# Router logits and prefix sums as 64-row halves, added on VectorE

## The chip, the cores and the metric

The kernel runs on one core of a Trainium2 chip. The metric is the device time of one execution in microseconds (us), the median of several. A core has five engines with a queue each: PE (TensorE: matmuls, with weight loads shown apart as PEld), DVE (VectorE), ACT (ScalarE), POOL (GpSimd) and SP (SyncE, here only issuing DMAs). Matmul results go to PSUM, eight banks of 2 KiB per partition.

## The reference

Two parts, one after the other. Attention without softmax, over 8 batches of 2816 tokens with 256 features and 64 query/key features:

```python
scores = (1.0 / S) * np.matmul(z, z.transpose(0, 2, 1))
attn = np.maximum(scores, 0.0) ** 2
x = (u * np.matmul(attn, v)).reshape(B * S, D)
```

Then a dense layer and a mixture of 8 experts, of which each token uses one:

```python
y_dense = np.maximum(x @ w1_dense, 0.0) @ w2_dense
logits = x @ w_gate                      # (22528, 8)
expert_idx = np.argmax(logits, axis=1)
gate_w = softmax(logits)[rows, expert_idx]
y[mask_e] = y_dense[mask_e] + gate_w[mask_e] * (np.maximum(x[mask_e] @ w1[e], 0.0) @ w2[e])
```

## The kernel before

The 22528 tokens are 176 blocks of 128. The attention takes them two at a time. For a query group of two or four blocks, `scores` multiplies z with itself into a pair of PSUM banks (L406); one of ACT and DVE applies the scaled relu (L421, L423) and one of ACT, DVE or, in the first groups, POOL squares into a bf16 tile `A` (L434, L436). `av` multiplies `A` with v into another pair of banks (L604), and DVE multiplies by u into `pays` (`gate_x`, L631). Since the query/key width is 64, z lies in SBUF twice, on rows 0 to 63 and on rows 64 to 127, and every matmul of the attention uses 64 rows of the 128x128 array: two matmuls stand side by side, one on each half of the rows, each with a PSUM bank of its own. The profile writes such a matmul as 64*128 and one over all rows as 128*128. v is used in the same halves, so a pair of L604 matmuls sums over 128 keys. There are four pairs of banks in the attention. `touch` is a tiny 64-row matmul by which `swap_rows` exchanges the two halves' banks in the middle of a block (L552).

For routing, the blocks form 18 chunks: 14 of 11 blocks, then 8, 6, 4 and 4. Each finished pair of blocks is transposed by a DMA on SP's queue into `xT` (L633). When a chunk is complete, `routing` runs in two steps put between the attention's matmuls. `logits` takes a pair of banks and does two matmuls per block, one for each 128 of the 256 features, with `xT` as weights and the eight router columns streamed (L660); `route_a` finds on DVE the largest logit and the one-hot choice `oh` (L670 to L680), and ACT takes the exponential. `route_pre` makes two 128-row matmuls of `oh` (L690, L691), with a matrix of ones and with a strict triangle; `route_b` turns them on DVE, in three functions `one`, `two`, `three`, into each token's place in its expert's list (L704 to L730). `scatter` then writes each block's rows to that place in DRAM by an indirect DMA on POOL (L748, L750). The last two chunks of 4 blocks are routed after the attention in PSUM tiles of another kind.

The order of the instructions on PE, ACT, DVE and SP is written out by a planner in the kernel while it is being built. It keeps an estimated time `now` along PE's work, and a time from which each other engine is free. Operations are offered with a readiness time, a rank and an estimated duration for each engine that may run them; the earliest possible start wins, then the lower rank. `route_a` and the three functions of `route_b` are such offers, for DVE alone, at ranks 0 and 0.5; relus have rank 1 and squares rank 4. Logits advance `now` by 0.6 us and the prefix sums by 0.25 us. A pair of banks goes back to the list when the last function that reads it is estimated to be done. On the chip the engines follow that order and wait on semaphores; the durations only shape the order.

After the attention, 90 slots (two more if the lists need them) fetch 256 sorted rows each, run the dense layer and the expert (L962, L970), combine on ACT and DVE (L985, L986), and POOL scatters the result into the output (L988).

Of the kernel before, what the change touches and what calls it, by code (L numbers as in the profile page):

```python
# [15 lines left out]
P = 128  # L16
# [3 lines left out]
def kernel(  # L20
# [12 lines left out]
    nc = tc.nc  # L33
    B, S, D = u.shape
    dq = z.shape[2]
    E = moe_w_gate.shape[1]
# [5 lines left out]
    G = 11  # L42
    sizes = [G] * (nB // G - 2) + [8, 6, 4, 4]
    starts = [sum(sizes[:q]) for q in range(len(sizes) + 1)]
    assert nK % G == 0 and starts[-1] == nB
    nQ = len(sizes)
# [37 lines left out]
    def banks(x, name, shape=(P, 2, 4 * P), dt=F32):  # L84

        return ps.tile(list(shape), dt, name=name, tag=f"b{x}")
# [4 lines left out]
    wg = const.tile([P, 2, E], BF, name="wg")  # L91
    w1d = const.tile([P, 2, F], BF, name="w1d")
    w2d = const.tile([P, 4, D], BF, name="w2d")
    ones = const.tile([P, P], BF, name="ones")
    ntri = const.tile([P, P], BF, name="ntri")
# [39 lines left out]
    now = [0.0]  # L135
# [5 lines left out]
    z_of, zn_of, zT_of, v_of, ut_of, xT_of, lg_of, rs = {}, {}, {}, {}, {}, {}, {}, {}  # L141
# [132 lines left out]
    for b in range(B):  # L274
        i = 0
# [14 lines left out]
    def offer(ready, rank, ways, then=None):  # L290
        count[0] += 1
        todo.append((rank, count[0], ready, ways, then))
# [91 lines left out]
    def take_pair():  # L384
        return pairs.pop(0)[1]

    def give_pair(t, x):
        pairs.append((t, x))
        pairs.sort()
# [249 lines left out]
    def vec(name, a, b=1, dt=F32, **kw):  # L639

        t = rt.tile([P, G * E if b > 1 else G], dt, name=name, **kw)
        return t[:, :a * b].rearrange("p (a b) -> p a b", b=b) if b > 1 else t[:, :a]

    bank_of = {}

    def small(q, name, shape):
        if q < nQ - 2:
            return banks(bank_of[q], name, shape)
        tag = "y" if q == nQ - 2 else "s"
        return late[tag].tile(list(shape), F32, name=name, tag=tag)  # L650

    def logits(q):
        n = sizes[q]

        lg = small(q, "lg", (P, G, E))
        lg_of[q] = lg[:, :n, :]
        for j in range(n):
            xT = xT_of.pop(starts[q] + j)
            for c in range(2):
                nc.tensor.matmul(out=lg[:, j, :], lhsT=xT[:, c, :],  # L660
                                 rhs=wg[:, c, :], start=(c == 0), stop=(c == 1))

    def bc(ap2):
        return ap2.unsqueeze(2).to_broadcast([P, ap2.shape[1], E])

    def route_a(q):
        n = sizes[q]
        lg = lg_of.pop(q)
        m = vec("m", n)
        nc.vector.tensor_reduce(out=m, in_=lg, axis=AX.X, op=ALU.max)  # L670
        d = vec("d", n, E)
        nc.vector.tensor_sub(d, lg, bc(m))
        ex = vec("ex", n, E)
        nc.scalar.activation(ex, d, AF.Exp)
        c = vec("c", n, E)
        nc.vector.scalar_tensor_tensor(out=c, in0=d, scalar=0.0, in1=desc8[:, :n, :],
                                       op0=ALU.is_ge, op1=ALU.mult)
        nc.vector.tensor_reduce(out=m, in_=c, axis=AX.X, op=ALU.max)
        oh = vec("oh", E, n, BF)
        nc.vector.tensor_tensor(out=oh.rearrange("p e t -> p t e"), in0=c,  # L680
                                in1=bc(m), op=ALU.is_equal)
        rs[q] = (oh, ex)
# [2 lines left out]

    def route_pre(q):
        oh, ex = rs[q]
        pre = small(q, "pre", (P, 2, E * G))
        pre = [pre[:, i, :E * sizes[q]].rearrange("p (e t) -> p e t", e=E) for i in range(2)]
        nc.tensor.matmul(out=pre[0], lhsT=ones[:], rhs=oh, start=True, stop=True)  # L690
        nc.tensor.matmul(out=pre[1], lhsT=ntri[:], rhs=oh, start=True, stop=True)  # L691
        rs[q] = (oh, ex, pre)

    first_of = [0]
# [1 line left out]
    def route_b(q):  # L696

        n = sizes[q]
        oh, ex, pre = rs[q]
        inc = vec("inc", E, n)  # L700

        def one():
            se = vec("se", n)
            nc.vector.tensor_reduce(out=se, in_=ex, axis=AX.X, op=ALU.add)  # L704
            o = starts[q] % (2 * G)
            rows = pays[:, o:o + n, :]
            nc.vector.reciprocal(rows.bitcast(F32)[:, :, P], se)
            nc.vector.tensor_copy(rows.bitcast(I32)[:, :, P + 1], tok[:, starts[q]:starts[q + 1]])
            assert q != Q1 or made_first[0]
            if first_of[0] != n:  # L710

                first_of[0] = n
                nc.vector.memset(smask[:, :E * n], 1.0)
                nc.vector.memset(smask[:, :E * n].rearrange("p (e t) -> p e t", e=E)[:, :, 0], 0.0)

        def two():
            tb = vec("tb", E, n)
            nc.vector.tensor_copy(tb, pre[0])
            nc.vector.tensor_add(tb[:, :, 0], tb[:, :, 0], base[:])
            nc.vector.tensor_tensor_scan(  # L720
                out=inc.rearrange("p e t -> p (e t)"), data0=smask[:, :E * n],
                data1=tb.rearrange("p e t -> p (e t)"),
                initial=0.0, op0=ALU.mult, op1=ALU.add)
            nc.vector.tensor_copy(base[:], inc[:, :, n - 1])

        def three():
            nc.vector.tensor_add(inc, inc, pre[1])
            nc.vector.tensor_mul(inc, inc, oh)
            pos = vec("pos", n, bufs=5)
            nc.vector.tensor_reduce(out=pos, in_=inc.rearrange("p e t -> p t e"),  # L730
                                    axis=AX.X, op=ALU.add)
            rs[q] = pos

        return [one, two, three]

    def nodep(ins, mine, *groups_):
# [26 lines left out]
    done = const.tile([P, E], F32, name="done")  # L763
# [283 lines left out]
    for b in range(B):  # L1047
        t = b * nK
# [30 lines left out]
    def chain(t, fns, then):  # L1079

        def done(t):
            if fns[1:]:
                chain(t, fns[1:], then)
            else:
                then(t)

        offer(t, 0.5, {"dve": (0.8, lambda eng: fns[0]())}, done)

    def routing(q):
        def first():  # L1090
            bank_of[q] = take_pair()
            logits(q)
            now[0] += 0.6
            offer(now[0] + 0.2, 0, {"dve": (1.3, lambda eng: route_a(q))}, middle)

        def middle(t):
            give_pair(t, bank_of[q])
            jobs.append((t + 2.5, second))

        def second():  # L1100
            bank_of[q] = take_pair()
            route_pre(q)
            now[0] += 0.25
            chain(now[0] + 0.2, route_b(q), last)

        def last(t):
            give_pair(t, bank_of[q])
            routed.append(q)
            waiting.extend(range(starts[q], starts[q + 1]))

        jobs.append((now[0], first))

    def late_routing(q):
        logits(q)
        route_a(q)

    def late_places(q):
        route_pre(q)
        for fn in route_b(q):
            fn()  # L1120
        waiting.extend(range(starts[q], starts[q + 1]))

    LAG = 5
    for q in range(nQ - 2):
        t = starts[q + 1] - 1 + LAG
# [40 lines left out]
    for s in range(NT - MAYBE + 2):  # L1166
# [4 lines left out]
        if s % 3 == 1 and waiting:  # L1171
# [5 lines left out]
    n = nc.values_load(used[0:1, 0:1], min_val=0, max_val=NH,  # L1177
                       skip_runtime_bounds_check_because="made by the table")
# [34 lines left out]
```

## Time and profile before

| | |
|---|---|
| median of 3 runs | 910.43 us (910.18 to 918.82) |
| the profiled execution | 923.2 us, its span 921.5 us, TensorE clock 0.997 |
| PE busy / DVE busy / ACT busy / POOL busy, whole span | 94% / 73% / 76% / 53% |
| first and last attention matmul (L604) | 10.1 us and 557.9 us |
| first matmul of the second part (L962) | 559.9 us |
| routing matmuls in the attention | 336 at L660, 16 at L690, 16 at L691 |

The profile lists instructions by source line. A line of the timeline has the start in us, the length in us, the engine, the line, what it writes and reads, the shape, and how many of the same were merged; in brackets stands the idle time before it and what ended that. A matmul's length contains its passage through the array, so matmuls that follow each other overlap; their pace is read from their starts.

### The profile page before, as it was taken

What the parts mean: (1) busy time and instruction counts of PE and PEld (TensorE: products, weight loads), DVE (VectorE), ACT (ScalarE), POOL (GpSimd) and SP (SyncE); (2) the same over time, 40 slices, a digit from 0 to 9 for tenths busy, and PEclk for the clock granted to TensorE, in tenths of its full rate; (3) what the DMA queues carried; (4) which work ended last, traced back from release to release, by engine and by line L of the source; (5) the groups of instructions that cost most, each with busy time, mean ns of one, the idle gap of its engine ahead of it and who ended that gap; (6) DMA issues with size and microseconds to landing.
All of it is one profiled execution on the core that took longest, in us unless ns stands there. A gap on an engine that the chain in (4) does not pass through costs nothing. (4 is left out here: it accounts for less than half of the span.)

```text
span 921.5 us, 30231 instructions
## 1 busy us (share of the span) xinstructions
PE 868.8 (94%) x12194; PEld 756.0 (82%) x12194; DVE 670.3 (73%) x1295; ACT 696.7 (76%) x868; POOL 485.7 (53%) x532
## 2 busy tenths in 40 slices
PE   7999999999999999999999998989988998999995
PEld 5898798788888888889888887778877887888785
DVE  7998889789889889789889966455634444445554
ACT  8988789789789779779779954567656666766664
POOL 8203353353343363353344344777777877876564
PEclk9999999999999999999999999999999999999998
DMA  9999999999999999999999964755544554443333
GB/s 178 159 198 159 187 189 178 186 185 181 208 161 195 192 185 177 201 183 179 195 167 157 162 129 92 124 123 108 113 102 99 117 110 100 111 101 93 87 90 76
DMA packets 291310, 136.80 MB, mean 148 GB/s; under 512 B 258910, under 2 KB 266334, under 8 KB 291168
## 3 DMA queue, kind: packets, MB, share of 16 engines
q1 hardware_dynamic: 263552, 79.40, 52.6%
q0 software_dynamic: 27616, 55.44, 26.8%
q8 instruction: 96, 1.57, 0.8%
q14 instruction: 46, 0.38, 0.2%
HBM read 61.54 MB, written 37.16 MB: 107 GB/s over the span
## 5 line engine op out<-in xcount | busy, mean ns | idle before, releaser
L604 PE MATMUL o<-vb,A 64*128 64x256 bf16 x7184 | 460.3, 269 | 3.2 <-POOL A L436 1.6
L604 PEld LDWEIGHTS <-A 64*128 64x128 bf16 x7184 | 379.1, 94 | 44.0 <-issue 3.4
L750 POOL DMA_INDIRECT xs<-pays,pi x176 | 192.0, 1091 | 271.9 <-DVE pi L748 218.4
L421 ACT ACTIVATE r<-s 128x1024 f32<-128x1024 f32 x252 | 249.7, 1018 | 40.0 <-PE s L406 33.7
L965 ACT ACTIVATE ring<-h_ps 128x1024 bf16<-128x1024 f32 x180 | 185.5, 1032 | 94.8 <-PE h_ps L962 50.2
L434 ACT ACTIVATE A<-r 128x1024 bf16<-128x1024 f32 (+1 forms) x234 | 238.3, 1045 | 8.2 <-DMA wall<-A 5.3
L986 DVE SCALAR_TENSOR_TENSOR ring<-yy,me,ring 128x256 f32<-128x256 f32 x180 | 86.2, 482 | 158.4 <-ACT ring L985 87.3
L436 DVE TENSOR_TENSOR A<-r 128x1024 bf16<-128x1024 f32 x155 | 187.0, 1220 | 4.6 <-ACT r L421 2.9
L988 POOL DMA_INDIRECT out_dram<-ring,me x140 | 146.1, 1044 | 67.5 <-DVE ring L986 35.4
L970 PEld LDWEIGHTS <-ring 128*128 128x128 bf16 x1440 | 139.9, 98 | 47.5 <-issue 31.9
L423 DVE TENSOR_SCALAR r<-s 128x1024 f32<-128x1024 f32 (+1 forms) x145 | 173.7, 1206 | 6.5 <-PE s L406 3.3
L406 PE MATMUL s<-zT 64*128 64x512 bf16 (+1 forms) x874 | 146.2, 355 | 5.3 <-ACT r L421 1.7
L970 PE MATMUL yy<-w2d,ring 128*128 128x256 bf16 x720 | 107.9, 272 | 24.5 <-DVE ring L986 22.8
L970 PE MATMUL yy<-ring 128*128 128x256 bf16 x720 | 108.0, 273 | 0.0
L962 PE MATMUL h_ps<-ring,w1d 128*128 128x256 bf16 x720 | 94.3, 272 | 3.5 <-DVE pays L631 1.8
L962 PE MATMUL h_ps<-ring 128*128 128x256 bf16 (+1 forms) x880 | 95.3, 253 | 1.4 <-issue 0.8
L985 ACT COPY ring<-yy 128x256 f32<-128x256 f32 x180 | 68.1, 378 | 37.2 <-PE yy L970 18.8
L950 DVE COPY ring<-wall 128x2048 bf16 x110 | 81.4, 755 | 14.5 <-issue 7.7
L962 PEld LDWEIGHTS <-ring 128*128 128x128 bf16 x880 | 73.4, 98 | 12.0 <-DVE ring L950 3.1
L631 DVE TENSOR_TENSOR pays<-o,ut 128x512 bf16<-128x512 f32 x88 | 60.4, 686 | 29.8 <-PE o L604 28.8
L962 PEld LDWEIGHTS <-w1d 128*128 128x128 bf16 x720 | 70.0, 98 | 12.2 <-issue 4.1
L406 PEld LDWEIGHTS <-zT 64*128 64x128 bf16 x874 | 54.9, 94 | 24.1 <-issue 13.7
(122 smaller groups left out, 444.8 us busy)
## 6 DMA issues: line engine op xcount, KB each, us to landing
ut<-in_u_dram SPq DMA_DIRECT2D x88, 256.0 KB
vb<-in_v_dram POOLq DMA_DIRECT2D x16, 384.0 KB
vb<-in_v_dram POOLq DMA_DIRECT2D x16, 320.0 KB
wall<-in_moe_w_dram POOLq DMA_DIRECT2D x16, 256.0 KB
xs<-pays,pi POOLq DMA_INDIRECT x176
zr<-in_z_dram POOLq DMA_DIRECT2D x7, 352.0 KB
out_dram<-ring,me POOLq DMA_INDIRECT x140
ring<-xs SPq DMA_TRANSPOSE x114
```

The source lines that it names most:

```text
L406: nc.tensor.matmul(out=s[:, h, y * c:(y + 1) * c], lhsT=zT[r, k + h, :], rhs=zT[r, i0:i0 + w, :], start=True, stop=True)
L421: nc.scalar.activation(r[:, :, :c], s[:, :, :c], AF.Relu, scale=1.0 / S)
L423: nc.vector.tensor_scalar(out=r[:, :, :c], in0=s[:, :, :c], scalar1=1.0 / S, scalar2=0.0, op0=ALU.mult, op1=ALU.max)
L434: nc.scalar.activation(a, r, AF.Square)
L436: (nc.gpsimd if eng == "pool" else nc.vector).tensor_mul(a, r, r)
L604: nc.tensor.matmul(out=o[:, j, 0:D], lhsT=block(n, k, i + j - i0)[r], rhs=v_of[b][r, k, :], start=(p == 0 and x == 0), stop=(p == 1 and x ...
L750: ins = nc.gpsimd.indirect_dma_start(out=xs, out_offset=bass.IndirectOffsetOnAxis(ap=pi[:], axis=0), in_=pays[:, g % (2 * G), 0:ROW].bitca ...
L962: nc.tensor.matmul(out=h_ps[:, f, hs, :], lhsT=w1(c, f), rhs=xT[:, hs, c, :], start=(c == 0), stop=(c == 1))
L965: nc.scalar.activation(h, h_ps[:].rearrange("p f h t -> p f (h t)"), AF.Relu)
L970: nc.tensor.matmul(out=y[:, k, :], lhsT=h[:, f, j * P:(j + 1) * P], rhs=w2(f), start=(f == 0), stop=(f == 3))
L986: nc.vector.scalar_tensor_tensor(out=ys, in0=y[:, 1, :], scalar=me[:, j, 0:1], in1=yd, op0=ALU.mult, op1=ALU.add)
L988: ins = nc.gpsimd.indirect_dma_start(out=out, out_offset=bass.IndirectOffsetOnAxis(ap=ids[j], axis=0), in_=ys, in_offset=None, bounds_chec ...
```

## The change

In the 16 chunks that are routed during the attention, each 128-row matmul of the logits and of the prefix sums becomes two 64-row matmuls, on rows 0 to 63 and 64 to 127. The first half writes to the first bank of the pair, the second to the second bank. VectorE adds the halves: for the logits a copy from PSUM and an add; for the sums with ones an add more; for the sums with the triangle an add more. The planner's estimate of `route_a` goes from 1.3 to 1.7 us and that of each function of `route_b` from 0.8 to 0.95 us. The last two chunks stay at 128 rows.

```diff
+    def halves(q):
+        return [slice(0, dq), slice(dq, 2 * dq)] if q < nQ - 2 else [slice(0, P)]
     def logits(q):
         n = sizes[q]
-        lg = small(q, "lg", (P, G, E))
-        lg_of[q] = lg[:, :n, :]
+        lg = small(q, "lg", (P, 1, G * E))
+        lg_of[q] = [lg[:, h, :n * E].rearrange("p (n e) -> p n e", e=E) for h in range(lg.shape[1])]
...
             for c in range(2):
-                nc.tensor.matmul(out=lg[:, j, :], lhsT=xT[:, c, :],
-                                 rhs=wg[:, c, :], start=(c == 0), stop=(c == 1))
+                for r, out in zip(halves(q), lg_of[q]):
+                    nc.tensor.matmul(out=out[:, j, :], lhsT=xT[r, c, :],
+                                     rhs=wg[r, c, :], start=(c == 0), stop=(c == 1))
     def route_a(q):
-        lg = lg_of.pop(q)
+        lg, *more = lg_of.pop(q)
         m = vec("m", n)
+        d = vec("d", n, E)
+        for part in more:
+            nc.vector.tensor_copy(d, lg)
+            nc.vector.tensor_add(d, d, part)
+            lg = d
         nc.vector.tensor_reduce(out=m, in_=lg, axis=AX.X, op=ALU.max)
-        d = vec("d", n, E)
         nc.vector.tensor_sub(d, lg, bc(m))
...
     def route_pre(q):
-        nc.tensor.matmul(out=pre[0], lhsT=ones[:], rhs=oh, start=True, stop=True)
-        nc.tensor.matmul(out=pre[1], lhsT=ntri[:], rhs=oh, start=True, stop=True)
+        for w, outs in zip((ones, ntri), pre):
+            for r, out in zip(halves(q), outs):
+                nc.tensor.matmul(out=out, lhsT=w[r, :], rhs=oh[r], start=True, stop=True)
...
         def two():
-            nc.vector.tensor_copy(tb, pre[0])
+            nc.vector.tensor_copy(tb, pre[0][0])
+            for part in pre[0][1:]:
+                nc.vector.tensor_add(tb, tb, part)
...
         def three():
-            nc.vector.tensor_add(inc, inc, pre[1])
+            for part in pre[1]:
+                nc.vector.tensor_add(inc, inc, part)
...
-        offer(t, 0.5, {"dve": (0.8, lambda eng: fns[0]())}, done)
+        offer(t, 0.5, {"dve": (0.95, lambda eng: fns[0]())}, done)
...
-            offer(now[0] + 0.2, 0, {"dve": (1.3, lambda eng: route_a(q))}, middle)
+            offer(now[0] + 0.2, 0, {"dve": (1.7, lambda eng: route_a(q))}, middle)
```

More of the change, by code (lines that the diff above doesn't have):

```diff
@@ L647, in small @@
         if q < nQ - 2:
-            return banks(bank_of[q], name, shape)
+            return banks(bank_of[q], name)
         tag = "y" if q == nQ - 2 else "s"
         return late[tag].tile(list(shape), F32, name=name, tag=tag)
+    def halves(q):
+        return [slice(0, dq), slice(dq, 2 * dq)] if q < nQ - 2 else [slice(0, P)]
     def logits(q):
         n = sizes[q]
-        lg = small(q, "lg", (P, G, E))
-        lg_of[q] = lg[:, :n, :]
+        lg = small(q, "lg", (P, 1, G * E))
+        lg_of[q] = [lg[:, h, :n * E].rearrange("p (n e) -> p n e", e=E) for h in range(lg.shape[1])]
         for j in range(n):
@@ L687, in route_pre @@
         oh, ex = rs[q]
[L688 to L691, printed above, removed]
+        pre = small(q, "pre", (P, 1, 2 * E * G))
+        pre = [[pre[:, h, i * E * G:i * E * G + E * sizes[q]].rearrange("p (e t) -> p e t", e=E)
+                for h in range(pre.shape[1])] for i in range(2)]
+        for w, outs in zip((ones, ntri), pre):
+            for r, out in zip(halves(q), outs):
+                nc.tensor.matmul(out=out, lhsT=w[r, :], rhs=oh[r], start=True, stop=True)
         rs[q] = (oh, ex, pre)
```

## Prediction

> **What bounds the kernel now.** I read first the page's busy times in 40 slices, to see which engine is full in which stretch.
>
> ```profile
> PE   7999999999999999999999998989988998999995
> ...
> DVE  7998889789889889789889966455634444445554
> ACT  8988789789789779779779954567656666766664
> ```
>
> The first 24 slices are the attention, and there PE is full. A busy PE isn't yet a PE at its pace, so the next views are the window from the first to the last attention matmul (columns: stretch, length, then the busy time and count of PE, PEld, DVE, ACT and POOL; granted clock, DMA share, GB/s), and the waits of PE up to 560 us (total, times, longest).
>
> ```profile
> 10.12:558.20 548.08, 536.28 (x9066) 468.22 (x9067) 481.29 (x888) 458.85 (x500) 223.18 (x225) 1.00 1.03 178
> ```
>
> ```profile
> PE d L552 <- ACT r L421: 2.0, 2, 1.7
> ...
> PE s L406 <- ACT r L421: 1.7, 7, 0.3
> PE o L604 <- POOL A L436: 1.6, 3, 0.9
> PE s L406 <- PE s L406: 1.5, 7, 0.3
> ...
> PE o L604 <- ACT A L434: 1.1, 2, 0.6
> ...
> PE o L604 <- DMA vb<-in_v_dram: 0.5, 1, 0.5
> PE pre L690 <- ACT r L421: 0.4, 1, 0.4
> PE s L406 <- DVE r L423: 0.4, 2, 0.2
> ```
>
> The clock is full, 1.00, and these waits sum to 9.2 us in 548: PE's own stream sets the length of the attention. DVE has 548.1 - 481.3 = 66.8 us to spare there, ACT 89.2 us. What the stream's pace is, and what the routing costs it, is read from the timeline around the first chunk, PE and then weight loads, and from the groups of the attention (the number behind the comma is the mean length in ns).
>
> ```profile
> 64.10 0.40 PE L604 MATMUL o<-vb,wall 64*128 64x256 bf16 x4
> 64.43 0.71 PE L660 MATMUL lg<-wg,xT 128*128 128x8 bf16 x22
> 65.07 2.36 PE L604 MATMUL o<-vb,A 64*128 64x256 bf16 x40
> ```
>
> ```profile
> 64.43 0.62 PEld L660 LDWEIGHTS <-xT 128*128 128x128 bf16 x22 [0.21 <-issue]
> ```
>
> ```profile
> L604 PE MATMUL o<-vb,A 64*128 64x256 bf16 x7134 | 456.9, 269 | 2.0 <-ACT A L434 1.1 <-POOL A L436 0.9
> ...
> L660 PE MATMUL lg<-wg,xT 128*128 128x8 bf16 x336 | 10.9, 167 | 0.0
> ...
> L660 PEld LDWEIGHTS <-xT 128*128 128x128 bf16 x336 | 9.5, 96 | 3.4 <-issue 3.4
> ```
>
> One L604 matmul lasts 269 ns; 40 of them, 20 pairs, start within 2.36 - 0.27 = 2.09 us, so a pair is due every 2.09 / 19 = 0.110 us. The two pairs from 64.10 give way at 64.32, but the next L604 starts at 65.07: the chunk's logits take 0.75 us of PE's time. A logit matmul lasts 167 ns, so 22 of them step by (0.71 - 0.167) / 21 = 0.0259 us, and 22 steps are 0.57 us. The other 0.18 us are the way in and out. "issue" says that PE waited for nobody there.
>
> That the gap belongs to the change of shape, not to a change of line or bank, shows where scores stand between L604 matmuls, all of 64 rows:
>
> ```profile
> 70.23 0.38 PE L604 MATMUL o<-vb,wall 64*128 64x256 bf16 x4
> 70.45 0.38 PE L406 MATMUL s<-zT 64*128 64x512 bf16 x2
> 70.67 0.60 PE L604 MATMUL o<-vb,wall 64*128 64x256 bf16 x8
> ```
>
> Two pairs of 256 columns, then one pair of 512, and each group starts 0.22 us after the last: no gap.
>
> **The change part by part.** *Logits, PE.* 22 matmuls of 128 rows become 44 of 64, in pairs on different rows. If the pairs stand side by side as the attention's do, 22 steps of 0.0259 us remain and the 0.18 us go, since no change of shape is left. In the smaller chunks the steps are fewer, and the way in and out is taken to be the same: 16 x 0.18 = 2.9 us saved. The pace of such short pairs isn't in the trace. Its bounds: one step a pair (2.9 us saved), or one step a matmul, which adds 22 x 0.0259 us to a full chunk. The nearest rows are what follows the prefix sums, weight loads and matmuls:
>
> ```profile
> 70.00 0.11 PEld L604 LDWEIGHTS <-A 64*128 64x128 bf16 x4
> ```
>
> ```profile
> 67.76 2.13 PE L604 MATMUL o<-vb,A 64*128 64x256 bf16 x36
> 69.82 0.21 PE L690 MATMUL pre<-oh,ones 128*128 128x88 bf16 x1
> 69.86 0.21 PE L691 MATMUL pre<-oh,ntri 128*128 128x88 bf16 x1
> 70.00 0.39 PE L604 MATMUL o<-vb,A 64*128 64x256 bf16 x4
> ```
>
> Four 64-row loads are done in 0.11 us. The 128-row ones, 96 ns each, step by (0.62 - 0.096) / 21 = 0.025 us, and four would take 3 x 0.025 + 0.096 = 0.17 us. Four matmuls of 0.27 us fit in 0.39, so with 0.110 between the pairs the two of a pair start within 0.01 us of each other. Loads and matmuls of the two halves run side by side, so I take the first bound.
>
> *Prefix sums, PE.* 36 matmuls from 67.76 are 18 pairs, due to give way at 67.76 + 18 x 0.110 = 69.74; the stream resumes at 70.00: 0.26 us per chunk. L691 starts 0.04 us after L690, so two pairs of halves are 0.08 us. Saved: 0.18 x 16 = 2.9 us, and with the logits **5.8 us**.
>
> *VectorE.* Four operations are added per chunk, a copy and three adds of 128x88. Their kinds are in these rows:
>
> ```profile
> 71.05 0.24 DVE L718 COPY tb<-pre 128x88 f32<-128x88 f32 x1
> ...
> 72.11 0.24 DVE L727 TENSOR_TENSOR inc<-inc,pre 128x88 f32<-128x88 f32 x1
> 72.39 0.25 DVE L728 TENSOR_TENSOR inc<-inc,oh 128x88 f32<-128x88 f32 x1
> 72.67 0.31 DVE L730 TENSOR_REDUCE pos<-inc 128x11 f32<-128x88 f32 x1
> ```
>
> A step of such a chain is 0.28 us from start to start, so a chunk has 4 x 0.28 = 1.1 us more, and 16 chunks 17.9 us (somewhat less in the two smaller ones). The maximum and the subtraction now read SBUF in place of PSUM, at no gain: the maximum L670 reads PSUM, L678 reads SBUF, and both take 241 ns.
>
> ```profile
> L670 DVE TENSOR_REDUCE m<-lg 128x11 f32<-128x88 f32 (+2 forms) x16 | 3.9, 241 | 19.3 <-PE lg L660 19.2
> L678 DVE TENSOR_REDUCE m<-c 128x11 f32<-128x88 f32 (+2 forms) x16 | 3.9, 241 | 0.6
> ```
>
> What hides this is the 66.8 us that DVE has idle, and ACT's 89.2, to which the planner can move relus and squares. Without that cover each microsecond is PE's. Behind the added operations stand, on DVE's queue, relus and squares (for which PE waits, through the banks and `A`), `gate_x` (for which the transposes to `xT` wait on SP's queue, and behind these SP's transposes of `A`), and the scatters' casts, for which POOL waits in any case. The logits' banks are last read by the second operation, the add, as they were by the subtraction, so they aren't held longer; those of the prefix sums are held two operations longer, 0.56 us.
>
> How much of DVE's routing reaches PE now? For this chunk it runs from 65.20 to 67.45 and from 71.05 to 72.67 + 0.31 = 72.98:
>
> ```profile
> 65.20 0.24 DVE L670 TENSOR_REDUCE m<-lg 128x11 f32<-128x88 f32 x1
> ...
> 67.38 0.07 DVE L714 MEMSET smask<- 128x8 f32 x1
> ```
>
> That is 2.25 + 1.93 = 4.2 us, 67 us in 16 chunks. The waits of PE for relus, squares and banks, without POOL's, are 2.0 + 1.7 + 1.5 + 1.1 + 0.4 + 0.4 = 7.1 us. If the routing caused all of them, 7.1 / 67 = 11% of a DVE microsecond would reach PE, 1.9 us of the 17.9. Bounds: nothing, if these waits come from elsewhere, and all 17.9. I take **1.5 us**, near the 1.9, because the planner's estimates grow too, by 0.4 + 3 x 0.15 = 0.85 us a chunk against 1.1, so it places other work around most of it.
>
> *The plan.* With other durations the planner picks other engines and places. That changes the 9.2 us of waits either way; I allow 3 us up and down.
>
> *After the attention.* The second part begins when the last `gate_x` is done:
>
> ```profile
> 559.92 1.03 PE L962 MATMUL h_ps<-ring,w1d 128*128 128x256 bf16 x8 [1.79 <-DVE pays L631]
> ```
>
> So what the attention saves moves the end by as much; the second part is unchanged.
>
> **The sum.** -5.8 + 1.5 = -4.3 us. The profiled execution took 923.2 us (its span 921.5 and 1.7 around it) and would take 918.9. It lies 12.8 us above the median of 910.43; where, one profile can't say, but the terms come from a stretch at full clock with a regular pace, so I take them off the median as they are: **906.1 us**.
>
> **The rivals.** *One step a matmul.* If the short halves follow each other, 672 steps of 0.0259 us are 17.4 us, where 336 steps and 2.9 us are 11.6 us now: 5.8 us more. The prefix sums have four steps of 0.04, 0.16 us in place of 0.26, and save 1.6. With DVE's 1.5 the sum is +5.7, 916.1 us. For it: no row has a long run of short 64-row pairs. Against it: the loads and starts at 70.00. Chance 15%. [...]
>
> *VectorE becomes what PE waits for.* If relus queue behind the routing and the banks run out, each of the 17.9 us that passes to PE counts in full. This is the rival on the other side: the loss decides from 5.8 / 17.9 = 32% on; with a half of it the time is 913.5 us, with all of it 910.4 - 5.8 + 17.9 = 922.5. For it: DVE is the fuller of the two engines that empty the banks. Against it: 11% is the most that the waits allow, and the longest of them isn't DVE's, as the next rows show. Chance of more than 32%: 17%, a third of that over 919.5 us.
>
> *The gain is given back at once.* The DMA engines, at a share of 1.03 in the window, hold the attention; then only DVE's 1.5 us count, 911.9 us. For it: PE's longest wait stands behind ACT, which had waited for a transposing DMA.
>
> ```profile
> 172.11 1.06 ACT L434 ACTIVATE A<-r 128x1024 bf16<-128x1024 f32 x1 [3.24 <-DMA wall<-A]
> ...
> 174.13 0.16 PE L552 MATMUL d<-ones 64*128 64x8 bf16 x1 [1.66 <-ACT r L421]
> ```
>
> Against it: that happens once, and PE's own waits for DMA are 0.5 us. The same time results if the change doesn't do what it says and the gaps stay with the 64-row halves, which the scores at 70.45 speak against. Chance together 11%.
>
> *A luckier plan.* The 5.8 us go and more than 3.3 us of the waits too: under 901.3 us. Chance 7%.
>
> **How the numbers follow.** The forecast, 906.1 with a range of its own of 901.5 to 910, has the remaining 50%. A change of 1% (9.1 us) is about what a measurement of this kernel can tell from none. Faster by over 1% is the luckier plan and a little of the forecast's edge, 8%; slower by over 1% is a third of the VectorE rival and the first rival with more waits, 10%; the rest, 82%, is within 1%. The range leaves out the luckier plan below and the upper half of the VectorE rival above: 901.5 to 917.
>
> **What would show it.** Right: 64-row logits with no "issue" gap ahead of their loads, the stream resuming 0.57 us after the pair before gave way, the attention ending near 554 us in the profile, DVE some 15 us busier in it. Wrong: logits that take 1.1 us a chunk; PE's waits for r, A or banks well over 9 us; or a shorter attention and a second part longer by as much.

## The result, and the profile after

The changed kernel takes **920.16 us** (median of 14 runs, 915.33 to 928.0); the kernel before, beside it on the same chip, takes 913.92 us (14 runs, 910.18 to 918.82). The ratio is 1.0065, with a 95% interval of 1.0039 to 1.009: slower by 0.65%, some 6 us, where 4.3 us less were forecast. The time lies above the range's upper end of 917 us. Two of the 12 runs of the kernel with only the logits halved, its profiled one among them, and one of the four runs of that kernel's attention fell into a slower state (894.66, 902.29 and 578.04 us), and the times given below leave them out.

The profiled execution of the changed kernel took 915.33 us, the lowest of its 14; that of the kernel before, 923.2 us, lies above all of its 14. So the two spans can't be held against each other; what PE does in each stretch can. First the window from the first attention matmul to the first matmul of the second part, and from there to the end, of the kernel before and then of the changed kernel (columns as in the prediction):

```profile
10.12:559.90 549.78, 536.28 (x9066) 468.22 (x9067) 482.01 (x890) 458.85 (x500) 223.50 (x225) 1.00 1.03 178
559.90:921.49 361.59, 325.55 (x3060) 283.05 (x3059) 181.46 (x395) 231.54 (x362) 254.29 (x288) 0.99 0.46 103
```

```profile
10.45:561.30 550.85, 533.77 (x9436) 477.56 (x9433) 493.16 (x951) 462.06 (x503) 251.07 (x224) 1.00 1.04 177
561.30:913.59 352.29, 324.80 (x3060) 284.21 (x3059) 183.84 (x396) 231.51 (x362) 255.18 (x289) 0.99 0.44 106
```

The attention is 1.1 us longer, though PE is busy for 2.5 us less in it and DVE for 11 us more. The second part, with the same matmuls in both, differs by 9.3 us between the two executions. That is about what runs of one kernel scatter by (9 and 13 us above), and it is why most runs below time the attention by itself.

The timeline of PE around the first chunk, in the changed kernel:

```profile
64.49 0.40 PE L604 MATMUL o<-vb,wall 64*128 64x256 bf16 x4
64.71 0.71 PE L665 MATMUL lg<-wg,xT 64*128 64x8 bf16 x44
65.26 1.92 PE L604 MATMUL o<-vb,A 64*128 64x256 bf16 x32
...
70.35 0.20 PE L702 MATMUL pre<-oh,ones 64*128 64x88 bf16 x2
70.39 0.20 PE L702 MATMUL pre<-oh,ntri 64*128 64x88 bf16 x2
70.42 0.38 PE L604 MATMUL o<-vb,wall 64*128 64x256 bf16 x4
```

Here the mechanism is the one that was forecast. 44 logit matmuls take 65.26 - 64.71 = 0.55 us, so a pair steps by 0.025 us, as one 128-row matmul did: halves run side by side. The gap at the change of shape is gone: counted as in the table below, this chunk takes 0.53 us of PE's time where it took 0.73. The prefix sums take 0.07 us where 0.26 were. But the same lines of another chunk, matmuls and then weight loads, read:

```profile
439.12 0.79 PE L665 MATMUL lg<-wg,xT 64*128 64x8 bf16 x43
440.42 0.16 PE L665 MATMUL lg<-wg,xT 64*128 64x8 bf16 x1 [0.52 <-issue]
440.43 0.40 PE L604 MATMUL o<-vb,A 64*128 64x256 bf16 x4
441.12 0.73 PE L604 MATMUL o<-vb,A 64*128 64x256 bf16 x10 [0.29 <-issue]
```

```profile
439.01 0.80 PEld L665 LDWEIGHTS <-xT 64*128 64x128 bf16 x43
440.39 0.09 PEld L665 LDWEIGHTS <-xT 64*128 64x128 bf16 x1 [0.58 <-issue]
440.43 0.22 PEld L604 LDWEIGHTS <-A 64*128 64x128 bf16 x5
441.13 0.55 PEld L604 LDWEIGHTS <-A 64*128 64x128 bf16 x11 [0.49 <-issue]
```

After 43 of the 44 matmuls PE stands still, with no semaphore to wait for, and its weight loads stand still too; it does five more matmuls and stands still again. The trace names no cause; the reading here is that PE has no instruction to do. In its waits the two entries with "issue" are new:

```profile
PE s L406 <- ACT r L421: 4.3, 12, 1.0
PE lg L665 <- issue: 2.6, 7, 0.5
PE o L604 <- issue: 2.1, 7, 0.5
...
PE o L604 <- ACT A L434: 1.3, 2, 0.7
```

The idle times of 2.6 and 2.1 us are counted from modelled ends. From start to start, the next table sums over the 16 chunks of the attention what a chunk takes of PE's time (from the attention matmul before to the one after, less the pace of 0.109 us), and over 15 to 545 us what PE's steps exceed their pace by 0.15 us or more: "dry" where neither the matmul nor its weight load waits on a semaphore, "waits" where one does.

| us | logits | prefix sums | dry (times) | waits |
|---|---|---|---|---|
| before | 11.27 | 4.96 | 0.2 (1) | 15.4 |
| changed | 13.68 | 1.36 | 6.4 (13) | 14.9 |

The prefix sums give 3.6 us, more than the 2.9 forecast. The logits, which should have gone to 8.4, rose to 13.7, because the 6.4 us of dry PE lie in them and just behind them.

### The profile page after: what moved, and what is told of

Its sections match the earlier page's. It is cut to its first block, busy times and chain, and to the rows that moved or that the text cites. A ratio compares the mean times of both kernels' runs of the same rounds, so it can differ in the third digit from the quotient of the medians.

```text
span 913.6 us, 31019 instructions
## 1 busy us (share of the span) xinstructions
PE 867.0 (95%) x12562; PEld 767.4 (84%) x12562; DVE 683.2 (75%) x1356; ACT 699.3 (77%) x871; POOL 514.5 (56%) x532
## 5 line engine op out<-in xcount | busy, mean ns | idle before, releaser
L604 PE MATMUL o<-vb,A 64*128 64x256 bf16 x7184 | 463.8, 269 | 4.5 <-issue 2.1
L604 PEld LDWEIGHTS <-A 64*128 64x128 bf16 x7184 | 387.0, 94 | 40.6 <-issue 7.3
L764 POOL DMA_INDIRECT xs<-pays,pi x176 | 221.6, 1259 | 260.6 <-DVE pi L762 178.0
L421 ACT ACTIVATE r<-s 128x1024 f32<-128x1024 f32 (+1 forms) x254 | 252.0, 1014 | 32.4 <-PE s L406 25.6
L436 DVE TENSOR_TENSOR A<-r 128x1024 bf16<-128x1024 f32 x154 | 184.4, 1215 | 2.6 <-ACT r L421 2.1
L964 DVE COPY ring<-wall 128x2048 bf16 x110 | 83.6, 775 | 11.2 <-issue 6.2
```

The costliest lines, as they stand in the source:

```text
L421: nc.scalar.activation(r[:, :, :c], s[:, :, :c], AF.Relu, scale=1.0 / S)
L436: (nc.gpsimd if eng == "pool" else nc.vector).tensor_mul(a, r, r)
L604: nc.tensor.matmul(out=o[:, j, 0:D], lhsT=block(n, k, i + j - i0)[r], rhs=v_of[b][r, k, :], start=(p == 0 and x == 0), stop=(p == 1 and x ...
L764: ins = nc.gpsimd.indirect_dma_start(out=xs, out_offset=bass.IndirectOffsetOnAxis(ap=pi[:], axis=0), in_=pays[:, g % (2 * G), 0:ROW].bitca ...
```

## The experiments

All kernels named `att_` end behind the attention: late routing, dense layer and experts are left out, and 128 rows of output are written. The runs fall into two groups. The whole kernel before took 877 to 878 us beside the first and 922 us beside the second, nearer to the 914 us of the result. In that second group, and in the result's own profiles, the attention, too, is 7 to 8 us longer by the traces; so each run is read against its own group. The chip's number on record doesn't tell the groups apart, 11 stands in both, so whether the chip makes the difference isn't known.

**Is it the attention?** The two attentions alone, the changed one twice.

> The kernel before, ended behind the last attention matmul: the late routing, the dense layer and the experts are left out, and only 128 rows of the output are written. It gives the attention's time by itself. From the profile of before (last attention matmul at 557.9 us) some 563 us by both theories.

> The changed kernel with the same part left out. If the attention is what became longer (theory: PE's queue of instructions runs dry in and behind the short 64-row logits, and the gaps of 0.4 to 0.7 us without a semaphore eat the gain of the prefix sums), it is 1 to 6 us over the attention of before. If the second part is what became longer (rival), the two attentions are equal within 1 us.

> The changed attention alone once more, as the measure for the runs beside it: 566 us if the chip is like the one before, 5 us over the attention of before.

Measured: 560.82 us (559.5 to 562.08) before, 566.35 (562.78 to 567.6) and 565.72 (562.86 to 568.66) changed. So the attention by itself carries a loss of 5 to 5.5 us. In this group the logits do shrink, 11.26 to 8.35 us, and the prefix sums from 5.24 to 1.34, a gain of 6.8 us, with one dry gap of 1.5 us. PE's waits on semaphores rise from 8.7 to 17.7 us instead, so the dry queue that was expected isn't what loses most of the time here. Before, then changed:

```profile
PE s L406 <- ACT r L421: 1.7, 6, 0.4
PE d L552 <- ACT r L421: 1.3, 1, 1.3
PE o L604 <- POOL A L436: 1.1, 2, 0.9
```

```profile
PE s L406 <- ACT r L421: 10.7, 19, 2.4
PE o L604 <- ACT A L434: 1.8, 2, 1.2
PE o L604 <- POOL A L436: 1.7, 3, 0.9
PE o L604 <- issue: 1.3, 1, 1.3
```

**Is it VectorE, the plan, the second bank?** `att_dve` keeps the matmuls at 128 rows, adds the four operations, with zeros from SBUF in place of the second half, and takes the change's estimates. The order on ACT, POOL and SP is then the changed kernel's. `att_twobank` lets the added operations read zeros from the second PSUM bank.

```diff
+            nc.vector.tensor_copy(d, lg)
+            nc.vector.tensor_add(d, d, nil[...])     # att_twobank: nil_of[q], a PSUM bank
```

> The attention of before with 128-row logits and prefix sums, but with the change's four VectorE operations per chunk (a copy and three adds, the adds with zeros) and its estimates for the planner, so its plan is the changed kernel's. If VectorE's 17.9 us and the plan are the cause (rival), it is as slow as the changed attention or slower, 3 to 8 us over before, since it lacks the gain on PE. If the dry queue is the cause (theory), it is 1 to 3 us over before and has no gaps without a semaphore.

> The attention with 128-row matmuls, VectorE's extra operations and the changed plan, the operands of the extra adds in the second PSUM bank, where one matmul each for the logits and for the prefix sums writes zeros. 64 instructions more on PE. Theory (instructions): 560 to 562 us. Rival (two banks, held and read): 565 us or more.

Measured: 560.33 us (560.0 to 561.97) and 560.41 (559.82 to 561.0), the time of `att_before`. The 16 x 1.1 us of DVE cost nothing, and neither does the bank. PE's waits for relus stay at 2.3 us:

```profile
PE o L606 <- POOL A L438: 2.4, 2, 1.5
PE s L408 <- ACT r L423: 2.3, 7, 1.0
PE o L606 <- ACT A L436: 0.8, 2, 0.6
```

**Which half?** Only the prefix sums halved, and only the logits.

```diff
 att_prefix: logits on all 128 rows into one bank, route_a estimated at 1.3
 att_logits: prefix sums on all 128 rows into one bank, one() estimated at 0.8
```

> The attention alone with the halves for the prefix sums only (and the estimate 0.95; the logits at 128 rows and 1.3). The gaps saved are 3.6 us. Theory now: every 256 PE instructions a refill of 16 KB holds up the other DMAs, and the 704 more instructions of the logits bring late transposes with them; the prefix sums add 64 only, so this one should be 2 to 4 us faster than the attention of before (560.8 us). Rival (two banks and their sums on VectorE cost the time): 1 to 3 us slower than before.

> The attention alone with the halves for the logits only. It saves 2.9 us of gaps and adds 672 instructions on PE. Theory (instructions): it is 5 to 9 us slower than before, the whole loss of the change and the missing gain of the prefix sums. Rival (banks and sums): 1 to 3 us slower, half of the loss.

Measured: 558.25 us (556.63 to 563.18) with the prefix sums, 567.0 (561.2 to 567.2, three runs) with the logits, where `att_before` took 560.82 elsewhere in the group. One half gains 2.5 us, the other loses 6.

**Is it the number of instructions?** `att_dup` is `att_dve` with every logit matmul done twice at 128 rows: 44 matmuls and 44 loads per chunk, as in the change, but in about 1.1 us.

```diff
-            for c in range(2):
+            for c in (0, 1, 0, 1) if q < nQ - 2 else (0, 1):
```

> The attention with 128-row matmuls, VectorE's extra operations and the changed plan (560.3 us), and every logit matmul done twice: as many PE instructions as the change has, 9.0 us more of PE's time, no 64-row halves and no second bank. By PE's time alone 569 us. Theory (instructions): 572 to 576 with waits for relus of 8 us and more. Rival (banks, halves): 569 with waits of some 2 us as without the doubles.

Measured: 567.15 us (566.46 to 571.33), 6.8 us above `att_dve`, less than the 8 us that 0.55 us more per full chunk make on PE. There is no dry gap, and the waits on semaphores are 6.8 us. In this group the number alone harms nothing. Whether it makes PE run dry can't be told from this run, since the change's own logits don't run dry in this group either.

**Is it that PE is faster, or that the burst is short?** `att_fill` puts 0.22 us of 64-row filler matmuls behind the logits and behind the prefix sums. `att_spread` puts one block's logits behind each pair of L604.

```diff
+            for _ in range(4):                       # att_fill
+                for h, r in enumerate(halves(q)):
+                    nc.tensor.matmul(out=t[:, h, 2 * P:3 * P], lhsT=ones[r, :], rhs=ones[r, :], ...)
-            logits(q)                                # att_spread
+            drip.extend(logits(q))
```

> The changed attention with PE's gain given back as work: four pairs of 64-row matmuls of ones, 128 columns each, 0.22 us, behind each chunk's logits and behind its prefix sums, into unused columns of the same banks. Everything else, the plan too, is the changed kernel's. If the faster PE is what runs into the late transposes (theory: the DMA engines are full, ACT's squares wait for transposing DMAs, PE for ACT's relus), it is faster than the changed attention by 3 to 6 us although PE does 7 us more. If the 64-row matmuls or the two banks as such cost the time (rival), it is 5 to 7 us slower than the changed attention.

> The changed attention with the logits spread out: one block's four 64-row matmuls behind each pair of L604 matmuls in place of a whole chunk at once. If the queue runs dry because 88 short instructions stand together (theory), the gaps without a semaphore go and the attention is 4 to 7 us shorter than the changed one. If the gaps come from late data, or the time from VectorE (rivals), it is within 2 us of the changed one.

Measured: 571.6 us (570.42 to 573.78) with filler: some 6 us of the filler's 7 (32 x 0.22) came on top of the 565.72 of `att_after2` beside it, and the waits stayed (15.1 us). So it isn't that a faster PE only meets the next limit. Spread logits took 564.25 us (564.16 to 565.47), 2 us better than in one burst, where 4 to 7 were expected; PE's waits for relus, 9.3 us, are many and short there (the longest 0.9), perhaps because the last logit, and with it ACT's exponential, comes later.

**Do the scatters' DMAs matter?** Both attentions without scatters and without the first fetches of the second part.

```diff
-        ins = nc.gpsimd.indirect_dma_start(out=xs, ...)
```

> The attention of before without the scatters to DRAM and the first three fetches, which relieves the DMA engines. By both theories 0 to 5 us under the attention of before.

> The changed attention without the scatters and the first three fetches. If full DMA engines turn PE's gain into waits (theory), the gain comes out now: 4 to 7 us under the attention of before without scatters. If the cause lies on the engines (rival), it stays 3 to 6 us over it.

Measured: 554.78 us (554.64 to 555.72) and 555.42 (550.83 to 558.36). Less traffic makes both faster. The changed kernel scatters by 7.5 us from run to run, the one before by 1: it has its gain in one run (550.83) and lost it in others. The trace of one of these others, 557.82 us, shows where. ACT's waits for transposing DMAs are nearly gone (the next section has them with the scatters), and PE's waits on ACT's relus are 3.0 us (10.7 with the scatters):

```profile
ACT A L434 <- DMA wall<-A: 0.7, 2, 0.4
```

```profile
PE o L604 <- issue: 4.6, 2, 3.9
PE s L406 <- ACT r L421: 3.0, 7, 1.2
```

Instead PE stands still twice without a semaphore, for 4.1 and 0.9 us, and around the end of the longer gap the granted clock drops to 0.50, for 6.8 us (columns as in the prediction):

```profile
271.62 0.61 PE L604 MATMUL o<-vb,wall 64*128 64x256 bf16 x4 [3.92 <-issue]
```

```profile
270.70:277.50 6.80, 5.88 (x52) 3.70 (x54) 3.63 (x13) 4.05 (x4) 0.00 (x0) 0.50 1.10 178
```

Held against `att_before_noscat` matmul by matmul, the changed kernel is 2.0 us ahead shortly before that gap and 4.3 behind some 20 us later. Without the two gaps and the halved clock it would take an estimated 557.8 - 6.3 - 0.9 = 550.6 us, the time of the best run. So by this one trace the late transposes go with the scatters, and most of the gain is there unless PE is left standing.

**Where it shows with late transposes.** With the same plan, `att_dve` and `att_after` can be laid side by side, matmul by matmul. The changed kernel gains 0.2 us at each logits and each prefix sum, and loses 0.4 to 2.6 us at one place in each of six batches, the scores shortly ahead of a prefix sum. For one of them, ACT and then PE of `att_after`:

```profile
239.32 1.06 ACT L434 ACTIVATE A<-r 128x1024 bf16<-128x1024 f32 x1 [3.26 <-DMA wall<-A]
```

```profile
241.34 0.61 PE L406 MATMUL s<-zT 64*128 64x512 bf16 x4 [2.42 <-ACT r L421]
```

and the same instructions of `att_dve`, without a wait:

```profile
235.14 1.06 ACT L436 ACTIVATE A<-r 128x1024 bf16<-128x1024 f32 x1
```

```profile
237.74 0.65 PE L408 MATMUL s<-zT 64*128 64x512 bf16 x4
```

ACT's square writes a tile of `A` that a transposing DMA still reads; the relus queue behind it, and PE behind the relus. In the lists ACT waits 11.3 us for these DMAs in the changed kernel, 1.6 in `att_dve` (and 5.1 in `att_before`):

```profile
ACT A L434 <- DMA wall<-A: 11.3, 6, 3.3
```

```profile
ACT A L436 <- DMA wall<-A: 1.6, 2, 0.9
```

**Pace, refills, plan.** The pages of the kernel before and the changed one list 96 and 99 packets of 16 KB that carry instructions:

```profile
q8 instruction: 96, 1.57, 0.8%
```

```profile
q8 instruction: 99, 1.62, 0.8%
```

They are read as the refills of PE: between 20 and 550 us one comes for every 128.1 and 128.3 matmuls with their loads in the mean, and 368 more matmuls in the whole kernel go with three more packets. Between 20 and 540 us the other queues start 190 DMA packets per 0.5 us in both traces; behind the start of such a packet it is in the mean 74 to 122 for some 1.5 us (before) and 85 to 123 for 2 us (changed), so they are slowed and not at a stand. `att_serial` does all upper halves of a chunk's logits before the lower ones, so that no neighbours run side by side. The two `shift` kernels move every refill by half a packet, 64 matmuls, against the work. `att_oldplan` gives the changed matmuls the old estimates.

```diff
 att_serial:   for r, out in zip(halves(q), lg_of[q]): for each block, for each c: matmul
 att_*_shift:  for _ in range(86): matmul of 32 columns  (was: 22 of 128)
 att_oldplan:  0.95 -> 0.8, 1.7 -> 1.3
```

> Attention only (the late routing, the dense layer and the experts are left out, 128 rows of output are written), the changed kernel with each chunk's logits in another order: first all upper halves, then all lower ones. No two neighbours stand on different rows, so a chunk should take 44 steps of 0.025 us, about 1.1 us, the pace of the run with doubled logits (567.15 us), with the 64-row form of the change (566.35 us). Theory that the short burst at double pace disturbs the supply (its instructions drain PE's queue and pull the refills ahead): the waits for relus vanish, and the time is that of the doubled logits less the prefix sums' 3.9 us, 562 to 565 us, with PE's waits for ACT's relus at about 2 us. Rival, the 64-row form itself: the waits stay at 9 to 11 us and 16 x 0.45 = 7 us of PE's time come on top: 571 to 574 us.

> Attention only, the changed kernel with 86 warm-up matmuls of 32 columns in place of 22 of 128 columns ahead of the attention: 128 PE instructions more, half of one 16 KB refill, in about the same 2.2 to 2.5 us. From there on every refill of PE's instructions falls 128 instructions earlier in the work. Theory that the loss is a matter of where the refills, behind each of which the other DMA queues stand still for 1.5 to 2 us, fall against the transposes: the time moves by 2 us or more from the 566 us of the changed attention, and the jumps at the scores ahead of the prefix sums become smaller or larger or move to other places. Rival, that the places don't matter: 565 to 567.5 us, with the same jumps.

> Attention only, the kernel with 128-row matmuls and the change's VectorE operations and plan (560.33 us), with the same 128 further PE instructions ahead of the attention. Theory that the places of the refills decide: this kernel, too, moves by 2 us or more, to 562 to 567 us, with PE's waits for ACT's relus well over its 2.3 us. Rival, that the places don't matter or that 128-row logits are safe wherever the refills fall: 559.5 to 561.5 us.

> Attention only, the changed kernel with the planner's two estimates of the kernel before (0.8 and 1.3 in place of 0.95 and 1.7), so that the plan is the one that the kernel before has. Theory that 64-row logits lose with any plan: 564 to 568 us. Rival, that the changed plan is what can't use the faster PE: the gain of 6.8 us less little, 554 to 557 us.

These four fell into the second group: 572.61 us (572.04 to 573.14), 572.26 (569.69 to 573.02), 571.22 (569.66 to 576.8) and 570.64 (569.07 to 572.05). The totals expected of them were those of the first group and can't be held against these; the traces can:

| us | logits | prefix sums | dry (times) | waits |
|---|---|---|---|---|
| att_dve_shift | 11.33 | 4.60 | 0 | 14.9 |
| att_after_shift | 11.89 | 1.35 | 6.3 (16) | 14.0 |
| att_oldplan | 12.65 | 2.52 | 5.7 (11) | 18.0 |
| att_serial | 15.15 | 1.35 | 3.1 (9) | 14.3 |

They resemble the result's own traces, in which the whole kernels have waits of 15 us too and the attention of the kernel before is as long as that of `att_dve_shift`. Every kernel with 64-row logits runs dry there, with either plan and wherever the refills fall; those with 128-row logits hardly do, `att_dve_shift` never and the kernel before once for 0.2 us. At half the pace (`att_serial`) PE runs dry for half as long. But 88 instructions in 1.1 us are no faster than the 44 in 0.57 us of 128-row logits: so it isn't the pace alone, and the number of short instructions in a row, or their 64-row form, counts too. The total is the same as for the double pace, though the logits themselves need 0.55 us more per full chunk. The rows of `att_after_shift`:

```profile
PE s L406 <- ACT r L421: 3.9, 11, 1.0
PE o L604 <- issue: 2.2, 7, 0.5
PE lg L665 <- issue: 1.6, 4, 0.6
```

and of `att_dve_shift`, which has no "issue" in its list:

```profile
PE s L408 <- ACT r L423: 5.2, 13, 0.9
PE s L408 <- PE s L408: 1.1, 5, 0.5
PE o L606 <- ACT A L436: 1.1, 2, 0.6
```

**The two halves in the whole kernel.**

> The whole kernel, with only the prefix sums as 64-row halves (their VectorE adds and the estimate 0.95 too); the logits stay at 128 rows and one bank, with 1.3. Theory that the loss belongs to the 64-row logits: the prefix sums' own gap, 0.23 to 0.24 us x 16 = 3.6 to 3.9 us, reaches the end at least in part, 1.5 to 4 us below the kernel before, a ratio of 0.9955 to 0.9985. Rival, that any microsecond that PE saves in the attention is given back with more: 1 to 4 us above it.

> The whole kernel, with only the logits as 64-row halves (their two VectorE operations and the estimate 1.7 too); the prefix sums stay at 128 rows and one bank, with 0.8. Theory that the loss belongs to the 64-row logits: 4 to 10 us above the kernel before, a ratio of 1.004 to 1.011, and above the kernel with halved prefix sums by 6 to 13 us. By the trace of the changed kernel PE should also run dry in or behind some of the logits, with gaps of 0.4 to 0.7 us for which no semaphore stands, or else wait longer for ACT's relus behind late transposes. Rival, that both halves together are needed for the loss: within 2 us of the kernel before.

Measured beside one kernel before (878.24 us, 23 runs): prefix sums alone **875.21 us** (872.69 to 880.12, 12 runs), ratio 0.9966, interval 0.9946 to 0.9986, faster; logits alone **881.95 us** (877.81 to 888.33, 10 runs), ratio 1.0055, interval 1.003 to 1.0081, slower. The mean granted clock of these 10 is 0.995 in the median, that of the kernel before 0.998; if PE's clock sets the time throughout, that is an estimated 0.003 x 880 = 2.6 us of the loss. The kernel with only the prefix sums halved beats both the kernel before and the one with halved logits. In its attention PE's waits are down to a few:

```profile
PE o L604 <- ACT A L434: 1.4, 2, 0.9
PE o L604 <- POOL A L436: 0.9, 1, 0.9
...
PE s L406 <- ACT r L421: 0.5, 2, 0.3
```

Its logits take 11.26 us, its prefix sums 1.11, no gap is dry.

## Why the prediction was wrong, point by point

**Logits, PE, 2.9 us saved: the step that failed.** Its bounds went by the array: one step a pair, or one step a matmul. The first was right, 0.025 us a pair, and the rival of one step a matmul is out. But the step costed the matmuls and not the supply of their instructions, which it put at nothing without a reason. 22 matmuls with their loads, 44 instructions in some 0.57 us, became 88 in 0.55 us, and in the result's trace PE stood still without a semaphore from 38 to 64 matmuls behind the burst's first. The logits then cost 2.4 us more than before instead of 2.9 less, and some gaps just behind come on top. That PE's queue was empty is the reading that fits; no run shows the queue itself. `att_serial` (same instructions at half the pace, half as long dry) says that the pace of the burst counts, and held against 128-row logits (the same pace, half the instructions, hardly dry) that it isn't the pace alone.

**Prefix sums, PE, 2.9 us saved: right.** Measured 3.6 us (4.96 to 1.36), and 3.0 us of the whole kernel's time when they are halved alone.

**VectorE, 1.5 us of 17.9 reaching PE: too much.** DVE was 11 us busier in the attention, and `att_dve` measured no cost. The rival in which VectorE becomes the wait, one of the two given for a slower kernel, falls with it, as one step a matmul did above: they had the right side by another mechanism. The 9.2 us of waits from which the term was worked out are counted from modelled ends; from start to start the kernel before has 15.4, and the changed one 14.9.

**The plan, 3 us either way.** `att_oldplan` and `att_dve` show no loss by the estimates, so nothing is left for this term.

**The gain is given back at once** was the nearest rival. Its chain, relus behind squares behind transposing DMAs, is what eats the gain in the first group, where PE seldom runs dry. Its price was wrong: it took the loss to end at VectorE's 1.5 us, and it went on to some 5 us. So the sum failed here at a second step, that what PE saves reaches the end: 6.8 us were saved, and 9 us of waits came in their place.

**After the attention.** The last attention matmul was to come near 554 us in the profile; it came at 559.8, and the second part's first matmul at 561.3. That the saving moves the end held for `prefix_full`. A second part of its own loss isn't seen: the attention alone carries the loss in the first group.

**The base of the sum.** The forecast was taken off a median of three runs, 910.43 us; the fourteen beside the changed kernel have 913.92. So 3.5 us of the distance are the base, and the change itself is +6.2 us where -4.3 was forecast: the sign is wrong with either base.

**What stays open.** Why 64-row logits make the transposes late in the first group isn't settled. Without the scatters they aren't late in the one trace; neither DVE, the bank, the plan nor the number of instructions does it alone, and slowing PE behind the burst doesn't mend it. In the result's trace the dry gaps turn an expected gain of 5.8 us into one near nothing; the attentions of the two profiled executions differ by 1.1 us, those of `att_after_shift` and `att_dve_shift` by 1.0 in the median, and where the rest of the 6 us goes in the 14 timed runs no trace shows. Longer gaps with a halved clock behind them, as in `att_after_noscat`, are one candidate that isn't tested. Why one group runs dry at the logits and the other doesn't isn't known either, and the two attentions of the result weren't run by themselves in the group that resembles it.

## What to carry to other kernels

When one matmul becomes two short ones side by side, cost their instructions beside the array's steps, how many stand in a row and how fast they are done: here 88 in 0.55 us in place of 44 in 0.57 went with 13 standstills of PE in the attention, 6.4 us, and the sign of them was an "issue" wait on matmuls and weight loads alike, with no semaphore. Halve the few long operations that cause a change of shape (here two matmuls per chunk, 3.0 us gained) and measure each half of a change alone; leave long runs of tiny ones whole (22 per chunk, halved, cost 3.7 us in `logits_full`). In `att_after` 6.8 us of PE's time were saved and 9 us of waits came in their place, so look for the wait that lies nearest behind.

## What the runs showed of the hardware

Where PE's longest waits without a semaphore lie in the first group, they come at a fixed place in the instruction stream: counted in matmuls of PE, at number 2399 in both runs of the changed attention, 2271 with filler, 8287 with the logits alone, 4575 and 5727 without the scatters. All are 95 above a multiple of 128, and the traces of before and after have one 16 KB packet for every 128 (128.1 and 128.3 in the mean). They last 0.2 to 4.1 us; the one in `att_after`:

```profile
148.39 0.51 PE L604 MATMUL o<-vb,A 64*128 64x256 bf16 x6
150.21 0.94 PE L604 MATMUL o<-vb,A 64*128 64x256 bf16 x14 [1.32 <-issue]
```

The packet ahead of it ended at 148.74 us, 1.5 us before PE went on; with the other five it is 1.2 to 1.6 us. So there, it seems, PE reached the end of a packet before the next was usable. No kernel with 128-row logits has such a gap in its trace. The gaps at the logits in the result's trace are of another kind: they lie at no such place.

A standstill came with more than its own length. In six traces (`att_prefix`, `att_logits`, `att_fill`, `att_after_noscat`, `att_after_shift`, `att_oldplan`) PE stands still for 1.4 to 4.3 us in the middle of the attention, in one piece or in two or three close together, with a semaphore or without, and around the end of that its granted clock drops to 0.50, for 3.4 us and in `att_after_noscat` for 6.8. A pair of L604 matmuls then takes 0.213 us in place of 0.109, so 3.4 us cost PE an estimated 1.7. The two profiled executions of the result have no such stretch in their attention.
